# Batch 5's x turned by four transfers in place of TensorE, and twenty steps moved up in a written-out order

## The chip, the cores and the metric

One core of a Trainium2 chip runs the whole kernel. The metric is the device time of one execution in microseconds (us). Five engines work side by side, each through its own list of instructions in order: TensorE (PE, matrix products, their results go to PSUM), VectorE (DVE), ScalarE (ACT), GpSimd (POOL), and SyncE (SP), which here only issues transfers (DMA). Engines wait for each other by semaphores.

## The reference

The kernel takes q, k and v, each 8 batches x 8 heads x 576 positions x 64, and four weight matrices. First comes an attention of two parts, then a mixing network on its result:

```
q_d, k_d, v_d = means of 4 neighbouring positions          # 144 positions
out_d  = softmax(q_d k_d^T / 8) v_d, each row repeated 4 times
out_l  = softmax(q k^T / 8 where |i - j| < 4) v             # a band
x      = out_d + out_l, heads side by side                  # 8 x 576 x 512
theta  = x @ w_theta
y      = w_tok_r @ (x * cos(theta)) + w_tok_i @ (x * sin(theta))
u      = x + y
out    = u + max(u @ w_ch, 0)
```

## The kernel before

**Order.** The kernel is a list of some 1,200 short words, ORDER (lines 57 to 97). Each word is a step: two letters for its kind, then a place (a PSUM bank, a staging slot or an engine: v is DVE, a is ACT, g is POOL). Every kind runs through its batches and chunks in turn, so the n-th `mk` of the list is known to be that of batch n // 3, chunk n % 3. This text writes it as mk 6.0: batch 6, chunk 0. Instructions get a dependency on the one before them on the same engine, so the list is the order of every engine, SP's transfers included; between engines only data and buffers order the work. A step that stands earlier in the list than another, on another engine, is not held by it.

**Steps of a batch that matter here.**

| kind | line | engine | what it does |
|---|---|---|---|
| lk, lq / lv, lw | 287 / 347 | SP | load of keys, queries / of the two halves of a chunk of v into a staging slot |
| ck, cq, cv | 295, 396 | any | cast of a staging slot to bf16 |
| tp, dk | 302, 306 | PE, SP | turns k and q (dk: by transfer, batch 7 alone) |
| ev | 312, 315 | any | puts the turned k or q in place |
| kd, qd | 321 to 335 | any | means of four (two instructions on POOL) |
| ps, ex, mk, po, nm | 482, 490, 503/505, 515, 523/524 | PE, ACT, any, PE, DVE | band scores, their exponential, the band as a mask, product with v, division |
| sd, ed, nd, xn, xd, xc | 426 to 470 | PE, ACT, PE, DVE, PE, any | the same for the means |
| xt, xa | 537, 545 | PE, DVE | turns the band's result back, adds the means' result: xT, x with channels on the partitions |
| th, cs / tt, ct, zt | 556, 561/562 / 568 to 577 | PE, ACT / PE, ACT, POOL | theta, cosine and sine for four chunks of 128 positions / for the last 64 |
| xm, zz | 595, 620 | PE, DVE | turns xT to x, 128 positions at a time (four 128x128 transposes into a PSUM bank); z = x times cosine and sine |
| dx, zz | 605, 615 | SP, DVE | the same for batches 6 and 7: one DMA transpose for each of the four blocks of channels (128x512, all positions), into halves of two staging slots; zz then reads SBUF |
| dz | 581 | SP | the last 64 positions of z by DMA transpose |
| mx, ua | 636, 641 | PE, DVE | nine products over positions; u = x + y in uT, eight pieces to a batch |
| du, ut | 645, 656 | SP, any | uT turned to ur by four DMA transposes; the last 64 positions kept aside |
| ch, rl, st | 666, 674, 680 | PE, DVE, SP | u @ w_ch; max(., 0) + ur into an output buffer; its store |
| ht, rt, ss, sr | 700 to 709 | PE, DVE, SP | the same for the last 64 positions of two batches at a time, two stores |

PSUM has eight banks. A step of TensorE names one or two, and waits until their last reader is done.

**Which batches take the DMA transposes** is line 46, and the two staging slots of each are read from the list's dx words: DXS holds them, and dx i goes to the slot i // 2 names.

```
XDMA = (6, 7)
def dx(b, i, w):
    x = (DXS[b][i // 2] > DXS[b][1 - i // 2])
    dc = 2 * x + i % 2
```

**Around the change.** SP's list near the middle of the last third reads, before: du 4.0, st 2.2, st 2.3, ss 1, st 3.0, du 4.1, st 3.1, dz 5, lw 7.3, lv 7.4, du 4.2, du 4.3, lw 7.4, st 3.2, dx 6.0. SP takes them one by one: a transfer that has to wait for its data holds all behind it. rl 4.0 on DVE needs all of du 4.

Of the kernel before, what the change touches and what calls it, by code (L numbers as in the profile page):

```python
# [42 lines left out]

NSTG = 16

XDMA = (6, 7)

RPE = (0, 1, 2, 3)
ZPE = (0, 1, 2, 3)
# [23 lines left out]
rl ckg ckg cvg cvg ch3 sd67 xt45 mkg ed rl ex ts mx0 xa xt67 po45 lv5 th1 cs xa nm ua tp23 th7 up4 up1 ucv xt56 xa mkv  # L73
lv4 ch0 eva po56 po23 cvg lq2 tt4 uca th1 cs th7 nm st nm xm2 lqb rl lq1 zz lqd ct cvg xm6 lw cqg ch5 cs zz cs cqa te
up0 up1 rl sd23 ucv po67 ch4 nm rl ch0 rl ucv tp67 lv7 ed cvg pv45 vdv lk8 lk9 eva st st tp23 eva xm0 ztg lk0 lka lw
xm1 zz zz zp7 ch6 zca lvc lv3 kdg nd45 xn nd23 ckg tp01 cva xn qdg utg mx7 cka ps23 rl kdg eva ps01 ua po45 mx6 up7 ex
ex lw lw lv8 nm qdg lw cqg po45 cqg ucv lvb lv2 lw sd23 sd01 lv5 ed mx7 lw lw ua tp23 nm xd4 ed ckg ckg xca st evv
tp01 eva mx6 mkg xt45 xt23 ua ua cva cvg cvg xt01 cka ts cvg xa xa mx7 th6 xa po45 nm pv23 tt0 th1 lk4 xm4 st st mkg
th5 vdv st cs nd23 ua zz ct cqg cqg ztg tp67 th4 cs dt po01 cs cs te xn evv po23 mx5 kdg qdg xm4 xm6 mx7 nm ps01 ex nm
ps23 ua lvd ua ex ch5 ps01 ex qdg zz lw lw xm7 zz rl kdg zp6 zz mkg nd23 xn lv1 lva lv3 mx5 zca sd67 lw ps01 ex po34  # L80
mx2 ua lw ed tp01 sd67 cva nm po34 eva cvv cvg ed lw up5 uca ua mx2 cvg nm cvg lvc xd3 ua pv04 xcv lk7 lk0 mx7 lq9 lq6
lq2 lqd lq8 lqb lq5 ckg ckg vda lq7 lw xt56 mkv cqg cqg po34 lk4 xt01 xa xa ch2 st cva ts lv6 th5 up6 ckg xm0 nm th1
tp34 cs ucv cs mkg rl eva mx6 ua ua th1 xt67 lk0 lk1 cs cqa po45 mkv xa nm ht3 rt tp67 th1 eva zz xm2 lv9 xm3 xm4 lw
lve zz zz ckg dk4 kdv mx0 cqg tp67 nd23 xn cs zz ua cqa eva mx1 nd67 xn cqa sr cqa cka tt2 ct dkb up4 cva cva ua mx0
mx7 ua cvg cvv uca te po01 nm qdg kdg qdg sd56 ed po23 ua ch4 rl xd0 ch1 ztg lw nm up7 ch4 uca xca po23 dz xt67 rl evg
ckg nm st st pv15 vda mx0 ps23 xa ex rl up1 up7 evg ua ucv mx6 uca ss ps01 ex xt45 cqa utg xa ua lv1 dk4 ps23 ex mx7
up0 uca th4 lvb sd56 mkv po23 lw lw xt01 utg dt ua dk7 cvv nm th7 du ed ts evg nd56 xa nd23 tt0 xn xn ct qdg mkv mkg
evv mx1 ztg xd2 up0 ua cs ch3 rl cs te mx4 ch7 qdg ps56 rl xcv ua mx1 ex cvg po23 po45 ua uca ps67 ex ht1 nm nm st st
rt cva ss mx0 ua po67 xt45 nm ps23 st xa ex ts du kdg th1 xm0 xm7 cs th6 cs xm4 zz zz zz ch5 rl kdg mx7 ua th0 po67 nm
cs te xt45 xa sd12 ch3 xm0 ch7 ch4 xt56 st ed sd12 mkg mkg ed ts zz dz lw mx0 lv1 du du cvv lw cvg th1 cs rl uta mx3  # L90
st rl rl xa dxb ua po45 po67 pv02 nm nm ua du mx1 vda ch4 dx mkg ua po23 po01 po67 rl sr nm mx5 ua mx4 tt5 dx1 du nm
nm nd23 xn nd01 st mx6 th7 mx2 cs xn xd3 mx0 ua ua xcv ua ua xt67 utv ct dx st st xt45 xt23 xa ch1 rl th0 ch6 ch1 ch7
cs xa xa tt0 zz zz th2 th3 cs st du du ch4 rl zz zz ztg ct dz rl mx2 mx0 mx1 cs ua ua st dxe dx ht0 ua th1 cs th3 dx7
dx zz st st mx2 rl mx1 ua ua cs zz dt mx3 mx1 mx2 zz zz ztg dz mx7 ua mx3 du du du mx6 rt ua ua utg ua st rl du st mx7
mx4 ua ua ua sr mx7 mx6 mx5 ua ua ua du du ua ch7 ch6 ss ch5 rl rl ch7 ch6 ch4 ch3 du du st uta dt sta rl st rl ht7
ch2 sta rl st rl sta rl st rt ssa sr rl sta rm su k0
# [4 lines left out]
def kernel(  # L101
# [490 lines left out]
    def xm(b, c, w):  # L592
        ps = at["xm", b, c] = bank16(w)[:, 0:DM]
        for dc in range(4):
# [3 lines left out]
    DXS = {b: [int(w[2:], 36) for w in ORDER.split() if w[:2] == "dx" and w[2:]][2 * i:2 * i + 2]  # L598
           for i, b in enumerate(XDMA)}
    stg16 = stga.bitcast(BF16)  # L600
# [12 lines left out]
    def zz(b, c, w):  # L613
        if b in XDMA:
            nc.vector.tensor_tensor(out=z[b % 2][:, 2 * c:2 * c + 2, :].rearrange("p r (k e) -> p r k e", k=2),
                                    in0=dxr(b, c).unsqueeze(1).to_broadcast([P, 2, 2, 256]),
                                    in1=cs[(4 * b + c) % NCS].rearrange("p r (k e) -> p r k e", k=2), op=ALU.mult)
            return
        x = at.pop(("xm", b, c))
        nc.vector.tensor_tensor(out=z[b % 2][:, 2 * c:2 * c + 2, :],  # L620
                                in0=x.unsqueeze(1).to_broadcast([P, 2, DM]),
                                in1=cs[(4 * b + c) % NCS], op=ALU.mult)
# [185 lines left out]
```

## Time and profile before

| what | us |
|---|---|
| three timed runs: median, lowest, highest | 231.33, 229.91, 231.4 |
| profiled execution: its span, the only time given of it | 232.2 |
| TensorE busy | 217.7 |
| DVE busy | 187.7 |
| ACT busy | 156.2 |
| POOL busy | 145.0 |
| granted TensorE clock, mean of the span | 0.993 of full |

A row of the profile's timeline reads: start in us from the span's start, duration in us, engine, line of the kernel, operation, output <- inputs, sizes, how many instructions are merged in the row; and in brackets the idle time of the engine just before it and what ended that. A row of the waits reads: the engine and line that waited, who ended it, then the sum in us, how often, the longest. A row of the chain: start, duration, what. SPq is SP's queue of transfers; for a transfer the duration is that of its issue on SP, not that of the data.

### The profile page before, as it was taken

The numbers are of one execution on the slowest core, as the hardware profiler recorded it, in microseconds if no ns is written. First come the engines' busy times: TensorE is split into PE (matmuls) and PEld (weight loads), VectorE is DVE, ScalarE is ACT, GpSimd is POOL, SyncE is SP. The second block draws the span as 40 slices with busy tenths as digits, with TensorE's granted clock in tenths as the row PEclk, the third lists the DMA queues.
The fourth block names the chain that finished last, engine by engine and source line by source line (L and its number), as shares of the span: only waits on it lengthen the run. The fifth ranks groups of instructions, "written<-read, shape, count | busy, mean of one in ns | idle before, by whom it ended". The sixth has DMA issues, their size and how long they took to land.

```text
span 232.2 us, 9404 instructions
## 1 busy us (share of the span) xinstructions
PE 217.7 (94%) x3943; PEld 152.6 (66%) x3970; DVE 187.7 (81%) x367; ACT 156.2 (67%) x243; POOL 145.0 (62%) x192
## 2 busy tenths in 40 slices
PE   7997899999999999899999989989998999999992
PEld 3655678877877666776775675756655775668741
DVE  5699888999988799789968887698986978558473
ACT  4589799689988898898877978778788232430000
POOL 7689977879985999879963489598952001100000
PEclk9999799999999999999999999999999999999999
DMA  6999968997999689968999996892284358656587
GB/s 217 395 390 390 291 114 238 361 300 118 265 391 179 165 245 285 243 142 214 205 165 347 307 213 115 206 153 92 67 149 109 71 127 193 138 159 137 142 227 245
DMA packets 76795, 49.41 MB, mean 213 GB/s; under 512 B 61136, under 2 KB 61392, under 8 KB 76752
## 3 DMA queue, kind: packets, MB, share of 16 engines
q1 hardware_dynamic: 76096, 47.76, 81.9%
q10 hardware_dynamic: 656, 1.05, 1.3%
q8 instruction: 31, 0.51, 0.9%
q14 instruction: 12, 0.10, 0.1%
HBM read 33.98 MB, written 9.44 MB: 187 GB/s over the span
## 4 chain that ended last, share of the span: by engine, by line
PE 60%; DMA 10%; POOL 10%; issue 6%; ACT 5%; DVE 4%; SPq 4%; DVEq 0%; POOLq 0%; ACTq 0%
PE PS L636 21%; PE PS L666 9%; PE PS L556 8%; DMA st<-in_q_dram 6%; PE PS L302 4%; POOL two L329 3%; PE PS L515 2%; SPq L347 2%; DMA st<-in_k_dram 2%; PE PS L537 2%; DMA ur<-uT 2%; POOL q_tm L295 2%; PE PS L482 2%; PE PS L447 1%; PE PS L595 1%
## 5 line engine op out<-in xcount | busy, mean ns | idle before, releaser
L636 PE MATMUL PS<-WT,z 128*128 128x288 bf16 x576 | 78.0, 287 | 0.0
L636 PEld LDWEIGHTS <-z 128*128 128x128 bf16 x576 | 53.9, 98 | 15.9 <-issue 1.3
L641 DVE TENSOR_TENSOR uT<-PS,xT 128x288 bf16<-128x288 f32 x64 | 28.6, 452 | 12.7 <-PE PS L636 10.9
L561 ACT ACTIVATE cs<-PS,pihc 128x512 bf16<-128x512 f32 x32 | 22.0, 689 | 21.1 <-PE PS L556 13.4
L556 PE MATMUL PS<-wth,xT 128*128 128x512 bf16 x116 | 30.8, 383 | 0.7 <-issue 0.2
L666 PE MATMUL PS<-wch,uT 128*128 128x512 bf16 (+1 forms) x122 | 29.8, 373 | 0.9 <-issue 0.6
L524 DVE TENSOR_TENSOR tmp<-PS,rl 128x512 bf16<-128x512 f32 x40 | 27.7, 692 | 1.4
L545 DVE TENSOR_TENSOR xT<-PS,xdT 128x928 bf16<-128x928 f32 (+1 forms) x24 | 22.3, 952 | 3.7 <-PE PS L537 2.3
L674 DVE SCALAR_TENSOR_TENSOR osb<-PS,ur 128x512 f32<-128x512 f32 x28 | 19.1, 687 | 7.1 <-DMA ur<-uT 3.0
L490 ACT ACTIVATE pm<-PS 128x1024 bf16<-128x1024 f32 (+1 forms) x24 | 20.5, 880 | 6.2 <-PE PS L482 6.1
L577 POOL TENSOR_TENSOR zT<-xT,cst 128x512 bf16<-128x512 bf16 x7 | 9.7, 1383 | 20.6 <-ACT cst L574 20.6
L295 POOL CAST k_tm<-st 128x576 bf16<-128x576 f32 x23 | 15.1, 668 | 11.2 <-DMA st<-in_k_dram 11.1
L396 POOL CAST v_w<-st 128x512 bf16<-128x512 f32 x21 | 13.3, 651 | 10.6 <-DMA st<-in_v_dram 10.5
L770 ACT ACT_TABLE_LOAD x15 | 19.2, 1283 | 0.3
L666 PEld LDWEIGHTS <-uT 128*128 128x128 bf16 x132 | 11.9, 98 | 11.2
L562 ACT ACTIVATE cs<-PS 128x512 bf16<-128x512 f32 x32 | 19.1, 597 | 0.0
L556 PEld LDWEIGHTS <-xT 128*128 128x128 bf16 x128 | 11.7, 99 | 10.6 <-issue 0.6
L295 POOL CAST q_tm<-st 128x576 bf16<-128x576 f32 x23 | 15.4, 686 | 4.9 <-DMA st<-in_q_dram 4.7
L503 POOL TENSOR_TENSOR pm<-pm,band 128x512 bf16<-128x512 bf16 x16 | 18.3, 1164 | 0.0
L329 POOL TENSOR_TENSOR two<-qT 128x576 f32<-128x576 bf16 x14 | 16.5, 1177 | 0.7 <-ACT qT L315 0.4
L620 DVE TENSOR_TENSOR z<-PS,cs 128x1024 bf16<-128x1024 bf16 x24 | 15.8, 684 | 0.5 <-ACT cs L562 0.3
L437 ACT ACTIVATE pd<-PS 128x864 bf16<-128x864 f32 x16 | 13.8, 889 | 2.5 <-PE PS L426 2.5
(124 smaller groups left out, 422.9 us busy)
## 6 DMA issues: line engine op xcount, KB each, us to landing
st<-in_k_dram SPq DMA_DIRECT2D x32, 288.0 KB, 6.5
st<-in_q_dram SPq DMA_DIRECT2D x32, 288.0 KB, 6.3
st<-in_v_dram SPq DMA_DIRECT2D x70, 128.0 KB, 5.2
out_dram<-osb SPq DMA_DIRECT2D x26, 256.0 KB, 4.0
st<-in_v_dram SPq DMA_DIRECT2D x4, 288.0 KB, 3.5
st<-in_moe_w_tok_r_dram SPq DMA_DIRECT2D x4, 288.0 KB, 6.5
st<-in_moe_w_tok_i_dram SPq DMA_DIRECT2D x4, 288.0 KB, 7.2
st<-in_moe_w_theta_dram SPq DMA_DIRECT2D x4, 256.0 KB, 6.7
```

Source lines behind the costliest of these rows:

```text
L295: COPY[w](out=to, in_=of)
L329: nc.gpsimd.tensor_tensor(out=t, in0=src[:, :, 0:2], in1=src[:, :, 2:4], op=ALU.add)
L490: nc.scalar.activation(out=pm[(3 * b + u) % NPM][:, :, 0:n].rearrange("p e c j w -> p e (c j w)"), in_=at.pop(("ps", b, u))[:, :, 0:4 * W ...
L524: nc.vector.tensor_tensor(out=tmp[(NCH * b + c) % NTMP].rearrange("p g (j d) -> p g j d", d=D), in0=ps[:, :, :, 0:D], in1=r.unsqueeze(3).t ...
L545: nc.vector.tensor_tensor(out=xT[b % 2][:, :, lo:lo + cnt].rearrange("p e (m j) -> p e m j", j=4), in0=at.pop(("xt", b, u))[:, :, 0:cnt].r ...
L556: nc.tensor.matmul(out=ps, lhsT=xT[b % 2][:, dc, P * c:P * c + P], rhs=wth[:, dc, :], start=(dc == 0), stop=(dc == 3))
L561: nc.scalar.activation(out=t[:, 0, :], in_=ps, func=AF.Sin, bias=pihc, scale=1.0)
L562: nc.scalar.activation(out=t[:, 1, :], in_=ps, func=AF.Sin, bias=0.0, scale=1.0)
L636: nc.tensor.matmul(out=ps, lhsT=z[b % 2][:, j, P * dc:P * dc + P], rhs=WT[:, j, cols], start=(j == 0), stop=(j == 8))
L641: nc.vector.tensor_tensor(out=uT[b % 2][:, dc, cols], in0=at.pop(("mx", b, i)), in1=xT[b % 2][:, dc, cols], op=ALU.add)
L666: nc.tensor.matmul(out=ps[:, cols], lhsT=uT[b % 2][:, dc, P * c:P * c + P], rhs=wch[:, dc, cols], start=(dc == 0), stop=(dc == 3))
L770: nc.scalar.activation(out=idle, in_=pihc, func=TABLE[kind])
```

## The change

Batch 5 is added to XDMA. With that its four xm steps on TensorE (xm 5.0 to 5.3, 16 transposes) go, four dx steps (dx 5.0 to 5.3) are added on SP, into staging slots 2 and 13, and zz 5.0 to 5.3 read those slots in place of PSUM banks. dx 5.0 to 5.3 stand in one row, between st 2.3 and du 4.1.

```
-XDMA = (6, 7)
+XDMA = (5, 6, 7)
...
-evv mx1 ztg xd2 up0 ua cs ch3 rl cs te mx4 ch7 qdg ps56 rl xcv ua mx1 ex cvg po23 po45 ua uca ps67 ex ht1 nm nm st st
-rt cva ss mx0 ua po67 xt45 nm ps23 st xa ex ts du kdg th1 xm0 xm7 cs th6 cs xm4 zz zz zz ch5 rl kdg mx7 ua th0 po67 nm
-cs te xt45 xa sd12 ch3 xm0 ch7 ch4 xt56 st ed sd12 mkg mkg ed ts zz dz lw mx0 lv1 du du cvv lw cvg th1 cs rl uta mx3
...
+evv mx1 cvg ztg xd2 up0 ua cs ch3 rl cs te mx4 ch7 qdg ps56 rl xcv ua mx1 ex po23 po45 ua uca ps67 ex ht1 nm nm st st
+rt cva dx2 dx dxd dx du lw lv1 lw st st ss du mx0 ua po67 xt45 nm ps23 xa ex ts kdg th1 cs th6 cs zz zz zz ch5 rl kdg
+mx7 ua th0 po67 cvv nm cs te xt45 xa sd12 ch3 ch7 ch4 xt56 ed sd12 mkg mkg ed ts zz dz mx0 du mkg cvg th1 cs rl uta
...
```

The other lines of the list change in the same way. What they amount to, engine by engine (all else keeps its place; TensorE's list only loses xm 5):

| engine | moved |
|---|---|
| ACT | ev 5.0 (first half of k) ahead of ck 5.2 |
| POOL | mk 5.0 in place of mk 5.1, ahead of ck 6.3; cq 6.3 and qd 6.0 ahead of ck 7.1 and cv 6.3; qd 7.0 ahead of the ev of the second half of k of batch 7; cv 7.1 ahead of zt 5; mk 7.2 ahead of cv 7.4 |
| DVE | mk 5.1 in place of mk 5.0; mk 6.0 ahead of xa 5.1 and ua 4.1; cv 7.3 ahead of nm 6.4, xa 6.1 and zz 5.3; xa 6.2 ahead of rl 4.0 and rl 4.1; zz 6.2 and zz 6.3 ahead of rl 5.0 |
| SP | after st 2.3: dx 5.0 to 5.3, du 4.1, lw 7.3, lv 7.4, lw 7.4, st 3.0, st 3.1, ss 1, du 4.2, dz 5, du 4.3, st 3.2 |

More of the change, by code (lines that the diff above doesn't have):

```diff
@@ L75 @@
 up0 up1 rl sd23 ucv po67 ch4 nm rl ch0 rl ucv tp67 lv7 ed cvg pv45 vdv lk8 lk9 eva st st tp23 eva xm0 ztg lk0 lka lw
-xm1 zz zz zp7 ch6 zca lvc lv3 kdg nd45 xn nd23 ckg tp01 cva xn qdg utg mx7 cka ps23 rl kdg eva ps01 ua po45 mx6 up7 ex
+xm1 zz zz zp7 ch6 zca lvc lv3 kdg nd45 xn nd23 ckg tp01 cva xn qdg utg mx7 eva cka ps23 rl kdg ps01 ua po45 mx6 up7 ex
 ex lw lw lv8 nm qdg lw cqg po45 cqg ucv lvb lv2 lw sd23 sd01 lv5 ed mx7 lw lw ua tp23 nm xd4 ed ckg ckg xca st evv
@@ L81 @@
 mx2 ua lw ed tp01 sd67 cva nm po34 eva cvv cvg ed lw up5 uca ua mx2 cvg nm cvg lvc xd3 ua pv04 xcv lk7 lk0 mx7 lq9 lq6
[L82 to L85, printed above, removed]
@@ L86 @@
-ckg nm st st pv15 vda mx0 ps23 xa ex rl up1 up7 evg ua ucv mx6 uca ss ps01 ex xt45 cqa utg xa ua lv1 dk4 ps23 ex mx7
-up0 uca th4 lvb sd56 mkv po23 lw lw xt01 utg dt ua dk7 cvv nm th7 du ed ts evg nd56 xa nd23 tt0 xn xn ct qdg mkv mkg
-evv mx1 ztg xd2 up0 ua cs ch3 rl cs te mx4 ch7 qdg ps56 rl xcv ua mx1 ex cvg po23 po45 ua uca ps67 ex ht1 nm nm st st
-rt cva ss mx0 ua po67 xt45 nm ps23 st xa ex ts du kdg th1 xm0 xm7 cs th6 cs xm4 zz zz zz ch5 rl kdg mx7 ua th0 po67 nm
-cs te xt45 xa sd12 ch3 xm0 ch7 ch4 xt56 st ed sd12 mkg mkg ed ts zz dz lw mx0 lv1 du du cvv lw cvg th1 cs rl uta mx3
@@ L91 @@
-st rl rl xa dxb ua po45 po67 pv02 nm nm ua du mx1 vda ch4 dx mkg ua po23 po01 po67 rl sr nm mx5 ua mx4 tt5 dx1 du nm
+lq2 lqd lq8 lqb lq5 ckg mkg ckg vda lq7 lw xt56 mkv cqg cqg po34 lk4 xt01 xa xa ch2 st cva ts lv6 th5 up6 ckg xm0 nm
+th1 tp34 cs ucv cs rl eva mx6 ua ua th1 xt67 lk0 lk1 cs cqa po45 mkv xa nm ht3 rt tp67 th1 eva zz xm2 lv9 xm3 xm4 lw
+lve zz zz cqg qdg ckg dk4 kdv mx0 tp67 nd23 xn cs zz ua cqa eva mx1 nd67 xn cqa sr cqa cka tt2 ct dkb up4 cva cva ua
+mx0 mx7 ua cvg cvv uca te po01 nm kdg qdg sd56 ed po23 ua ch4 rl xd0 ch1 ztg lw nm up7 ch4 uca xca po23 dz xt67 rl evg
@@ new lines @@
+ckg nm st st pv15 vda mx0 ps23 xa ex rl up1 up7 evg ua ucv mx6 uca ss ps01 ex xt45 cqa utg mkv xa ua lv1 dk4 ps23 ex
+mx7 up0 uca th4 lvb sd56 po23 lw lw xt01 utg dt ua dk7 cvv nm th7 du ed ts qdg evg nd56 xa nd23 tt0 xn xn ct mkv mkg
+evv mx1 cvg ztg xd2 up0 ua cs ch3 rl cs te mx4 ch7 qdg ps56 rl xcv ua mx1 ex po23 po45 ua uca ps67 ex ht1 nm nm st st
+rt cva dx2 dx dxd dx du lw lv1 lw st st ss du mx0 ua po67 xt45 nm ps23 xa ex ts kdg th1 cs th6 cs zz zz zz ch5 rl kdg
+mx7 ua th0 po67 cvv nm cs te xt45 xa sd12 ch3 ch7 ch4 xt56 ed sd12 mkg mkg ed ts zz dz mx0 du mkg cvg th1 cs rl uta
@@ L92 @@
+mx3 st xa dxb rl rl ua po45 po67 pv02 nm nm ua du mx1 vda ch4 dx ua po23 po01 po67 rl sr nm mx5 ua mx4 tt5 dx1 du nm
 nm nd23 xn nd01 st mx6 th7 mx2 cs xn xd3 mx0 ua ua xcv ua ua xt67 utv ct dx st st xt45 xt23 xa ch1 rl th0 ch6 ch1 ch7
-cs xa xa tt0 zz zz th2 th3 cs st du du ch4 rl zz zz ztg ct dz rl mx2 mx0 mx1 cs ua ua st dxe dx ht0 ua th1 cs th3 dx7
+cs xa xa tt0 zz zz th2 th3 cs st du du ch4 zz zz rl ztg ct dz rl mx2 mx0 mx1 cs ua ua st dxe dx ht0 ua th1 cs th3 dx7
 dx zz st st mx2 rl mx1 ua ua cs zz dt mx3 mx1 mx2 zz zz ztg dz mx7 ua mx3 du du du mx6 rt ua ua utg ua st rl du st mx7
```

## Prediction

> **What bounds the kernel now.** I read the page first, then who waits for whom on TensorE from 108 us on (the stretch that the edits reach), then the engines in order of time around each wait found. Steps are named kind, batch, index: po 6.0 is the po step of batch 6, chunk 0. A row is matched to its step by counting the steps of that line along the order list.
>
> ```profile
> span 232.2 us, 9404 instructions
> PE 217.7 (94%) x3943; PEld 152.6 (66%) x3970; DVE 187.7 (81%) x367; ACT 156.2 (67%) x243; POOL 145.0 (62%) x192
> ```
>
> TensorE is busy for 94% of the span. So from 108 us on the time falls only where TensorE's list gets shorter or where one of its few idle pieces goes. The idle pieces, by who ended them:
>
> ```profile
> PE PS L515 <- DVE pm L505: 0.8, 1, 0.8
> PE PS L302 <- POOL q_tm L295: 0.8, 1, 0.8
> PE PS L515 <- DVE osb L674: 0.4, 1, 0.4
> PE PS L515 <- DVE xT L545: 0.3, 1, 0.3
> PE PS L426 <- POOL qd L335: 0.3, 1, 0.3
> ```
>
> These five are 2.6 us. I leave out the rest of that answer, pieces put down to issue, of which no edit is the cause. Every number below is set against the profiled 232.2 us; the median of the timed runs, 231.33 us, lies 0.9 us below it, and a gain counted in the profile is taken off that median.
>
> **The change part by part.** *tp 6.1 (the second half of q), 0.81 us, and sd 6, 0.3 us.* TensorE waits for a cast that POOL makes behind another cast, ck 7.1, for which a key load lands late.
>
> ```profile
> 121.08 4.92 SPq L287 DMA_DIRECT2D st<-in_q_dram  x8
> 121.08 4.99 DMA st<-in_q_dram
> 134.20 0.66 POOL L295 CAST k_tm<-st 128x576 bf16<-128x576 f32 x1 [3.83 <-DMA st<-in_k_dram]
> 135.53 0.68 PE L302 MATMUL PS<-ident,q_tm 128*128 128x128 bf16 x9 [0.81 <-POOL q_tm L295]
> ```
>
> POOL's 134.20 cast is ck 7.1, and cq 6.3 stands behind it. The load of cq 6.3 is the fourth of the eight issues from 121.08, so out by about 124.0 at the latest (four issues at the mean of 0.62 us end at 123.5); the first landed 4.99 us after its issue, which puts the fourth near 129, five microseconds before it is used. The new list puts cq 6.3 and qd 6.0 ahead of ck 7.1, into the 3.83 us in which POOL stands. The 0.81 us go; qd 6.1, which ended the 0.3 us wait, comes earlier too, as qd 6.0 has then been done in the idle time. mk 5.0 and mk 5.1 change engines, each into the other's kind of place: no TensorE wait of the list above is on either, so nothing.
>
> *po 6.0, 0.83 us.* It waits for mk 6.0 on DVE.
>
> ```profile
> 150.54 1.12 DVE L545 TENSOR_TENSOR xT<-PS,xdT 128x928 bf16<-128x928 f32 x1 [1.34 <-PE PS L482]
> 151.94 1.88 DVE L505 TENSOR_TENSOR pm<-pm,band 128x1024 bf16<-128x1024 bf16 x1
> 157.81 0.68 DVE L505 TENSOR_TENSOR pm<-pm,band 128x1024 bf16<-128x1024 bf16 x1
> 151.10 2.18 POOL L312 COPY kT<-st 128x1152 bf16<-128x1152 bf16 x1 [2.58 <-DMA st<-k_tm]
> 153.88 0.32 PE L515 MATMUL PS<-v_w,pm 64*64 64x65 bf16 x16 [0.83 <-DVE pm L505]
> ```
>
> The same form takes 0.68 us for mk 6.1 and 1.88 us here: it starts inside POOL's copy, which ends at 153.28, and ends 0.54 us after that. The new list has mk 6.0 ahead of xa 5.1, in DVE's idle 1.34 us, before that copy starts. The 0.83 us go. What may still hold it there is qd 7.0, moved into POOL's 2.58 us; but po 6.0 asks only at about 153, some three microseconds after mk 6.0 can start.
>
> *The sixteen transposes, 0.89 us.*
>
> ```profile
> 167.22 0.61 PE L595 MATMUL PS<-ident,xT 128*128 128x128 bf16 x8
> 167.67 1.03 PE L556 MATMUL PS<-wth,xT 128*128 128x512 bf16 x4
> 168.53 0.39 PE L595 MATMUL PS<-ident,xT 128*128 128x128 bf16 x4
> 168.75 1.03 PE L666 MATMUL PS<-wch,uT 128*128 128x512 bf16 x4
> ```
>
> From start to start eight take 0.45 us and four take 0.22 us; the last four (xm 5.3) are priced like these, 0.22: 0.89 us of a busy TensorE. The Trainium skill ("VectorE: DVE Perf Modes", The three transpose paths and Rules for kernel authors) advises against this edit: it gives 390 ns for a 128x128 on TensorE, 1309 ns on the transfer path, and says to use TensorE where PSUM will do. By that figure sixteen would free 6.2 us, an estimate that this trace's 0.22 us per four does not bear out.
>
> *The four transfers on SP's queue, and the wait behind them.* They stand behind st 2.3 and ahead of du 4.1, lw 7.3, lv 7.4, lw 7.4, st 3.0, st 3.1, ss 1, du 4.2, dz 5, du 4.3.
>
> ```profile
> 155.60 0.61 DVE L545 TENSOR_TENSOR xT<-PS,xdT 128x448 bf16<-128x448 f32 x1
> 155.66 1.98 SPq L680 DMA_DIRECT2D out_dram<-osb  x2
> 165.81 0.54 SPq L709 DMA_DIRECT2D out_dram<-osb  x1
> 167.03 1.28 SPq L645 DMA_TRANSPOSE ur<-uT  x1
> 170.85 1.34 SPq L347 DMA_DIRECT2D st<-in_v_dram  x2
> 172.24 2.62 SPq L645 DMA_TRANSPOSE ur<-uT  x2
> 173.66 4.26 DMA ur<-uT
> 178.04 1.29 DVE L674 SCALAR_TENSOR_TENSOR osb<-PS,ur 128x512 f32<-128x512 f32 x2 [2.11 <-DMA ur<-uT]
> 179.91 0.45 PE L515 MATMUL PS<-v_w,pm 64*64 64x65 bf16 x31 [0.34 <-DVE xT L545]
> 198.29 5.92 SPq L605 DMA_TRANSPOSE st<-xT  x4
> DMA to landing us min/median/max: 2.4/3.0/4.1
> ```
>
> SP stands from 157.64 to 165.81, since ss 1 waits for DVE's rt 1 and everything else for batch 4 is behind ss 1. The transfers need the whole xT of batch 5, which xa 5.2 completes at 156.21, so they fill that gap: four took 5.92 us for batch 7 (the last two rows; the landing row is line 605's own). Then, in the old clock, 157.64 + 5.92 = 163.56; du 4.1 1.28, the three v halves 3 x 0.67, st 3.0 and 3.1 1.98 as st 2.2 and 2.3 took, ss 1 0.54, du 4.2 1.31, dz 5 1.28 as du 4.1: du 4.3 is reached at 172.0. Before, it was issued at 173.66 and landed 4.26 us later. Now it lands at 176.2 even with that, 1.7 us earlier. DVE's rl 4.0 stands idle 2.11 us for it until 178.04, and that is what TensorE's po 7.0 waits on (0.4 + 0.3 us: rl 4.1, and xa 6.2 behind it). The new list also puts xa 6.2 ahead of rl 4.0. What is late next is DVE itself, which was free for rl 4.0 at 175.93 (178.04 - 2.11) and comes to it at 176.5 with xa 6.2 (0.6 us) done: both rl end 1.29 us later, at 177.8. TensorE, which asked about 0.7 us before 179.91, asks 0.89 us earlier now, at 178.3. The 0.7 us go.
>
> *ev 5.0 ahead of ck 5.2: nothing.*
>
> ```profile
> 95.61 0.46 PE L482 MATMUL PS<-qT,kT 64*64 64x64 bf16 x32 [0.60 <-ACT kT L315]
> 95.23 0.69 DVE L674 SCALAR_TENSOR_TENSOR osb<-PS,ur 128x512 f32<-128x512 f32 x1 [0.93 <-DMA out_dram<-osb]
> 96.64 0.69 DVE L524 TENSOR_TENSOR tmp<-PS,rl 128x512 bf16<-128x512 f32 x1
> 97.56 0.32 PE L515 MATMUL PS<-v_w,pm 64*64 64x65 bf16 x16
> ```
>
> The 0.60 us go there, but rl 1.2 on DVE still waits for a store until 95.23, nm 3.3 behind it still ends at 97.33, and po 3.4, which takes over its PSUM pair, can start only 0.2 us earlier. Without that cover it would be worth 0.6 us; that end goes into the range.
>
> *zz 5 from SBUF.* Its operands were PSUM and SBUF, now both are SBUF, and POOL is at work on mk 7 then.
>
> ```profile
> 166.77 4.49 POOL L503 TENSOR_TENSOR pm<-pm,band 128x512 bf16<-128x512 bf16 x4
> 169.71 0.69 DVE L620 TENSOR_TENSOR z<-PS,cs 128x1024 bf16<-128x1024 bf16 x1 [0.33 <-ACT cs L562]
> 195.60 1.28 DVE L615 TENSOR_TENSOR z<-st,cs 128x1024 bf16<-128x1024 bf16 x2
> ```
>
> From PSUM it ran undisturbed beside POOL (0.69 us); from SBUF it takes 0.64 us with POOL idle; beside POOL no row shows it. The nearest row is mk 6.0 above: such a multiply stands until POOL's instruction ends. Per zz the cost is between 0 and one POOL piece, 4.49 / 4 = 1.12 us. A gain is excluded, since undisturbed times are alike. zz 5.2 has 0.33 us of cover. I take one half piece, 0.56 us, that reaches TensorE through rl 3.2 (xt 6.1 takes its PSUM bank).
>
> Sum: 0.81 + 0.3 + 0.83 + 0.89 + 0.7 - 0.56 = 2.97 us, in the profile 232.2 - 3.0 = 229.2, in the timed median **228.3 us**. After po 7.0 the lists of TensorE, and SP's queue from du 5.0 on, are paced by TensorE's own mx steps, so what is won by then is kept.
>
> **The rivals.** *The port.* zz 5.0 and zz 5.2 each stand a full piece: 2.24 - 0.33 = 1.9 us late, and TensorE's xt 6.1 with them. The gain left is 3.5 - 1.9 = 1.6 us, 229.7 us. For it: mk 6.0's 1.88 us, and POOL goes back to back for 4.49 us. Against it: waits that were won earlier shift DVE and POOL alike, and once DVE has its turn it made mk 6.1 and the next copy in a row. The Trainium skill ("SBUF — State Buffer", Who interferes with whom) has a rule for it: a DVE instruction with two SBUF inputs and a POOL instruction that reads SBUF exclude each other for the whole of the one that is first. The row of mk 6.0 agrees.
>
> *Other waits take their place.* The first three edits win nothing lasting, for instance as batch 7's loads, set by SP, hold the casts: only 0.89 + 0.7 are left, 229.7 us. For it: POOL's 3.83 us is a load's landing, and that does not move. Against it: of the five waits only the two of batch 6 stand behind that landing, and the new list takes them out from behind it.
>
> *Slower: the queue.* If SP stood at each transfer until it has landed, four would take 4 x 4.1 = 16.4 us in place of 5.92, and du 4.3 would go 10.5 us later, at 182.5; landed 4.26 us later, 186.7, it holds rl 4.0 8.7 us longer than before, of which the 1.94 us won earlier come off: +6.8, 238.1 us. It decides from 9.6 us for the four on (du 4.3 then lands 1.94 us later than before, which is no change); with the median 3.0 each, 12.0 us, it gives +2.4, 233.7 us. Against it: batch 7's four were issued in 5.92 us, less than two landings.
>
> That the change does not do what it says is no case here: the switch drops the four xm steps from the list and turns zz's operand with them.
>
> **How the numbers follow.** About 1%, 2.3 us, is what can be told from no change: 229.0 to 233.6. The forecast, with the gain between 2.3 and 4.1 us (0.6 more from ev 5.0, none lost at the port), gets 0.60 and is faster. The port gets 0.20 and the other waits 0.14, both within 1%. The queue gets 0.06, slower by more than 1% in most of it. With a little of the rivals on the better side: faster 0.61, same 0.34, slower 0.05. The range runs from 231.33 - 4.1 = 227.2, a little under for the spread of single runs, 227.0, up to 230.9, past both rivals at 229.7 by the 1.2 us at which their worst pieces meet; 0.13 is left above and 0.06 below.
>
> **What would show it.** In the profile after: no wait of TensorE on q_tm near 134 us; mk 6.0 at 0.7 us and no wait of po 6.0; no L595 between 160 and 180 us; the four L605 before ss 1, in about 5 to 6 us; du 4.3 landing before DVE reaches rl 4.0; po 7.0 about 3 us earlier. The port would show as line 615 rows of over 1 us beside POOL's L503 and as idle time of TensorE ahead of xt 6.1 (L537). What would make me wrong: cv 7.3, now ahead of nm 6.4 on DVE, standing for its load lw 7.3; or a later stage that does not keep what po 7.0 wins.

## The result and the profile after

Six timed runs of the changed kernel have a median of 233.46 us (232.46 to 234.0), six of the kernel before, on the same chip, 229.91 us (229.21 to 231.4). The ratio is 1.0127 with a 95% interval of 1.0092 to 1.0163: the change makes the kernel slower by 1.3%, 2.1 to 3.7 us. The forecast was 228.3 us, and the range ended at 230.9. (The ratios in this text are taken over fast executions and need not be the quotients of the medians beside them.)

The page of the changed kernel, and who waits for whom on TensorE from 108 us on (engine, line, who ended the wait, then us, times, longest):

```profile
span 230.7 us, 9407 instructions
PE 218.5 (95%) x3954; PEld 151.2 (66%) x3954; DVE 187.9 (81%) x367; ACT 156.1 (68%) x243; POOL 146.2 (63%) x192
```

```profile
PE PS L515 <- DVE uT L641: 1.9, 1, 1.9
```

All five waits of before are gone. The steps behind four of them, tp 6.1, mk 6.0, po 6.0 and po 7.0, from the timeline:

```profile
134.28 0.67 PE L302 MATMUL PS<-ident,q_tm 128*128 128x128 bf16 x9
...
147.44 0.69 DVE L505 TENSOR_TENSOR pm<-pm,band 128x1024 bf16<-128x1024 bf16 x1
...
151.26 0.30 PE L515 MATMUL PS<-v_w,pm 64*64 64x65 bf16 x16
...
177.59 0.45 PE L515 MATMUL PS<-v_w,pm 64*64 64x65 bf16 x32
```

None waits, and mk 6.0 takes 0.69 us in place of 1.88. But one wait has come: a po step (line 515) stands 1.9 us for a ua step of DVE (line 641). And the profiled span is 1.5 us shorter than that of before (232.2), although the timed runs are longer. Both facts turn out to matter. The rows around the new wait, from the timeline of the changed kernel:

```profile
155.13 5.16 SPq L605 DMA_TRANSPOSE st<-xT  x4
162.53 2.00 SPq L347 DMA_DIRECT2D st<-in_v_dram  x3
163.48 5.46 POOL L503 TENSOR_TENSOR pm<-pm,band 128x512 bf16<-128x512 bf16 x4
168.90 1.60 POOL L505 TENSOR_TENSOR pm<-pm,band 128x512 bf16<-128x512 bf16 x1
165.67 3.81 DVE L615 TENSOR_TENSOR z<-st,cs 128x1024 bf16<-128x1024 bf16 x3 [0.26 <-DMA st<-in_v_dram]
169.41 0.68 DVE L674 SCALAR_TENSOR_TENSOR osb<-PS,ur 128x512 f32<-128x512 f32 x1
170.01 0.44 DVE L641 TENSOR_TENSOR uT<-PS,xT 128x288 bf16<-128x288 f32 x1
168.39 0.21 PE L515 MATMUL PS<-v_w,pm 64*64 64x65 bf16 x1
170.50 0.32 PE L515 MATMUL PS<-v_w,pm 64*64 64x65 bf16 x15 [1.90 <-DVE uT L641]
```

The four transfers are issued in 5.2 us, well ahead of need. Then zz 5.0 to 5.2 (line 615) take 3.81 us in a row, beside POOL's mk 7.0, 7.1 and 7.2 (lines 503 and 505). In the old form, from PSUM, they took 1.28 + 0.69 us with 0.33 us between them; the first two, in the trace of the kernel before:

```profile
168.10 1.28 DVE L620 TENSOR_TENSOR z<-PS,cs 128x1024 bf16<-128x1024 bf16 x2
```

Behind them on DVE stand rl 3.2 and ua 4.7, and po 6.4 on TensorE takes the PSUM bank that ua 4.7 releases. Line 615 alone, in the changed kernel:

```profile
L615 DVE TENSOR_TENSOR z<-st,cs x4: 681/1164/1647, 165.7 to 172.9; 128x1024 bf16<-128x1024 bf16 x4
```

The same instruction takes 0.68 us or 1.65 us. The two long ones, zz 5.1 and 5.2, are beside POOL and end about 0.55 us after a piece of POOL's does. zz 5.0 is beside POOL too, but it starts 0.02 us ahead of POOL's third piece and takes 0.69 us. POOL pays as well: its four pieces take 5.46 us in place of the 4.49 of before. So the two engines stand for each other in turn.

### The profile page after: what moved, and what is told of

Read it like the earlier page. It is cut to its first block, busy times and chain, and to the rows that moved or that the text cites. A ratio compares the mean times of both kernels' runs of the same rounds, so it can differ in the third digit from the quotient of the medians.

```text
span 230.7 us, 9407 instructions
## 1 busy us (share of the span) xinstructions
PE 218.5 (95%) x3954; PEld 151.2 (66%) x3954; DVE 187.9 (81%) x367; ACT 156.1 (68%) x243; POOL 146.2 (63%) x192
## 4 chain that ended last, share of the span: by engine, by line
PE 74%; DMA 6%; DVE 6%; POOL 5%; ACT 4%; issue 2%; SPq 0%; DVEq 0%; POOLq 0%; ACTq 0%
PE PS L636 27%; PE PS L556 11%; PE PS L666 9%; PE PS L302 5%; DMA st<-in_q_dram 3%; PE PS L515 2%; PE PS L537 2%; POOL two L329 2%; PE PS L447 2%; PE PS L764 2%; PE PS L482 2%; DVE z L615 2%; DMA utr<-ut 2%; PE PS L595 2%; PE PS L568 2%
## 5 line engine op out<-in xcount | busy, mean ns | idle before, releaser
L556 PE MATMUL PS<-wth,xT 128*128 128x512 bf16 x128 | 31.8, 379 | 0.0
L666 PE MATMUL PS<-wch,uT 128*128 128x512 bf16 (+1 forms) x132 | 31.2, 373 | 0.5 <-POOL wch L243 0.5
L503 POOL TENSOR_TENSOR pm<-pm,band 128x512 bf16<-128x512 bf16 x16 | 19.2, 1226 | 0.0
L329 POOL TENSOR_TENSOR two<-qT 128x576 f32<-128x576 bf16 x14 | 16.0, 1145 | 4.4 <-ACT qT L315 4.2
L329 POOL TENSOR_TENSOR two<-kT 128x580 f32<-128x580 bf16 x13 | 15.0, 1152 | 0.6 <-ACT kT L315 0.2
L315 ACT COPY kT<-PS 128x1152 bf16<-128x1152 bf16 x11 | 12.3, 1121 | 3.8 <-PE PS L302 3.3
```

What stands on the lines that cost most here:

```text
L329: nc.gpsimd.tensor_tensor(out=t, in0=src[:, :, 0:2], in1=src[:, :, 2:4], op=ALU.add)
L503: EW[w].tensor_tensor(out=t[:, x], in0=t[:, x], in1=m[:, x], op=ALU.mult)
L556: nc.tensor.matmul(out=ps, lhsT=xT[b % 2][:, dc, P * c:P * c + P], rhs=wth[:, dc, :], start=(dc == 0), stop=(dc == 3))
L666: nc.tensor.matmul(out=ps[:, cols], lhsT=uT[b % 2][:, dc, P * c:P * c + P], rhs=wch[:, dc, cols], start=(dc == 0), stop=(dc == 3))
```

## The experiments

For each kernel the table gives the time between the ends of steps on DVE, from its one trace: E is the start to ua 2.0; then the stretches ua 2.0 to ua 3.7, to rl 3.1, to ua 4.6, to ua 4.7, to nm 7.0, to ua 7.7; and the sum from ua 2.0 on. Every edit but ev 5.0's lies behind ua 2.0; E varies between 94.3 and 97.5 us among kernels that are, but for ev 5.0, the same there. So traces are compared by the sum, and times by the ratio to the kernel before.

| kernel | E | to ua 3.7 | to rl 3.1 | to ua 4.6 | to ua 4.7 | to nm 7.0 | to ua 7.7 | sum |
|---|---|---|---|---|---|---|---|---|
| before, the trace of the prediction | 96.29 | 46.55 | 19.31 | 4.17 | 5.06 | 9.84 | 39.41 | 124.34 |
| before (e0) | 96.80 | 45.10 | 18.67 | 4.17 | 5.06 | 9.81 | 39.41 | 122.23 |
| before (e11) | 95.80 | 45.11 | 17.71 | 4.17 | 5.06 | 10.00 | 39.41 | 121.47 |
| before (e12) | 97.46 | 45.09 | 17.72 | 4.17 | 5.06 | 9.79 | 39.41 | 121.25 |
| changed | 96.22 | 45.35 | 17.71 | 4.25 | 6.91 | 8.45 | 39.41 | 122.08 |
| changed (e4) | 95.17 | 45.25 | 17.71 | 4.22 | 8.10 | 8.45 | 39.40 | 123.14 |
| changed (e13) | 96.50 | 45.52 | 17.72 | 4.17 | 8.03 | 9.98 | 39.41 | 124.84 |
| changed (e14) | 95.64 | 45.19 | 17.71 | 4.17 | 8.03 | 10.02 | 39.41 | 124.53 |
| moves only (e7) | 94.33 | 45.19 | 17.72 | 4.17 | 5.18 | 8.87 | 39.41 | 120.53 |
| moves only (e1) | 95.12 | 45.19 | 17.61 | 4.17 | 5.15 | 8.78 | 39.41 | 120.31 |
| moves only (e9) | 96.28 | 45.23 | 17.61 | 4.17 | 5.17 | 8.86 | 39.40 | 120.45 |
| transfers only (e2) | 94.33 | 45.23 | 17.70 | 4.17 | 7.49 | 12.96 | 39.41 | 126.97 |
| cv 7.4 ahead of mk 7.0 (e3) | 94.72 | 45.24 | 17.61 | 4.17 | 5.61 | 8.45 | 39.40 | 120.49 |
| the same, near slots (e8) | 96.89 | 45.19 | 17.76 | 4.17 | 5.06 | 8.45 | 39.40 | 120.03 |
| changed, near slots (e10) | 96.02 | 45.19 | 17.61 | 4.17 | 6.93 | 10.07 | 39.40 | 123.37 |
| stand added (e6) | 96.84 | 45.20 | 17.69 | 4.17 | 7.26 | 8.61 | 39.41 | 122.33 |
| transfers further ahead (e5) | 94.32 | 45.20 | 17.61 | 5.82 | 6.01 | 8.45 | 39.41 | 122.50 |

The theories: that the gains of the prediction were in one execution only (against: they are real and something larger eats them); that zz 5 from SBUF is locked out by POOL; that TensorE's stand costs more than its length, through the granted clock; and that the slots which the transfers were given add a wait of their own.

### The kernel before, again

The first kernel is the one before, without any edit, timed and traced once more; the later two executions, e11 and e12, were each timed once.

> The kernel before, unchanged, for a second trace of it. Theory A (the trace the prediction was read from is a late execution, and its waits of TensorE at 134, 153 and 179 us are not those of most executions): the ratio is 1.00, the span of most runs lies 227 to 230 us, and the new trace lacks at least two of the three waits (0.81, 0.83 and 0.7 us). Theory B (the waits are always there, and the change loses more than them elsewhere): the same three waits stand in the new trace within 0.3 us each.

Ratio 1.003 (0.9987 to 1.0074), so the comparison itself is even. TensorE's waits from 108 us on in this trace, issue left out:

```profile
PE PS L515 <- DVE pm L505: 0.6, 1, 0.6
...
PE PS L515 <- DVE osb L674: 0.4, 1, 0.4
PE PS L515 <- DVE xT L545: 0.3, 1, 0.3
```

tp 6.1's 0.8 us and sd 6's 0.3 us are not there; of the three waits that the expectation names, one is gone and two stay, so neither theory's condition is met in full. This execution took 232.33 us with a span of 230.6, so the device time is the span and about 1.7 us more; the changed kernel's is the same (232.46 and 230.7). The span of 232.2 on which the prediction was built then belongs to an execution of about 233.9 us, later than every one of the three timed runs of 229.91 to 231.4.

> The kernel before, for a third trace: which waits are in its executions. Theory E (the waits at tp 6.1 and po 6.0 come and go from one execution to the next, the one at po 7.0 is in all): no wait of TensorE at tp 6.1, between 0 and 0.8 us at po 6.0, 0.7 us at po 7.0; from ua 2.0 to ua 7.7 it takes 121 to 122.3 us (124.3 and 122.2 in the two traces so far).

> As e11: a fourth trace of the kernel before. Theory E: from ua 2.0 to ua 7.7 121 to 122.3 us, the 0.7 us at po 7.0 again.

230.6 and 232.03 us. All waits of TensorE in e11 from 108 us on:

```profile
PE PS L515 <- DVE osb L674: 0.5, 1, 0.5
PE PS L515 <- DVE xT L545: 0.3, 1, 0.3
```

e12 has 0.3 and 0.3. So po 6.0's wait for mk 6.0 is 0.83, 0.6, 0 and 0 us in four executions of one kernel, and the two of tp 6.1 and sd 6 are in one of four. Only po 7.0's, 0.6 to 0.8 us, is in all. The stretch to ua 3.7 is 45.1 us in all three later traces of this kernel, against the 46.55 of the prediction's.

### The moves alone

The changed kernel with batch 5's x on TensorE, as before:

```
-XDMA = (5, 6, 7)
+XDMA = (6, 7)
...
-rt cva dx2 dx dxd dx du lw ...
+rt cva du lw ...
...
-... th1 cs th6 cs zz ...
+... th1 xm0 xm7 cs th6 cs xm4 zz ...
...
-... sd12 ch3 ch7 ...
+... sd12 ch3 xm0 ch7 ...
```

> The twenty moves without the transfers: batch 5's x stays on TensorE. Theory A (the waits that the moves take away are not there in most executions): ratio 0.995 to 1.01. Theory C (the moves do win their 1.9 us and the transfers lose more): ratio 0.985 to 0.993. Theory D (the loss comes from the moves): ratio 1.01 to 1.015, as for the whole change.

> e1 again, on the same chip as e4 to e6. All theories: ratio 0.990 to 1.000. Theory E (the moves take away waits that are only in part of the executions of the kernel before, at po 6.0, and one that is in all, at po 7.0): 0.5 to 1.5 us under the kernel before, and a narrower spread of its times.

> The moves alone (e1, e7) once more, beside e8 and e10: ratio 0.992 to 0.999. It is the measure for e8: if TensorE's shorter list is worth anything once port and slots are out of the way, e8 lies under it.

Ratios 0.9974 (0.9934 to 1.0014), 0.9948 (0.9907 to 0.9989) and 0.9943 (0.9911 to 0.9975): the moves gain 0.3 to 0.6%, 0.6 to 1.3 us (e1's interval reaches no change, those of the other two do not). TensorE has no wait left from 108 us on but pieces put down to issue. By the traces the sum is 120.31, 120.53 and 120.45 us, a mean of 120.43, against 121.36 for e11 and e12 (e0, where po 6.0 still waits 0.6 us, has 122.23). Those 0.93 us lie in the one stretch from ua 4.7 to nm 7.0, 8.8 to 8.9 us for 9.8 to 10.0: that of po 7.0.

### The transfers alone

```
-XDMA = (6, 7)
+XDMA = (5, 6, 7)
...
-rt cva ss mx0 ua po67 xt45 nm ps23 st xa ex ts du kdg th1 xm0 xm7 cs th6 cs xm4 zz zz zz ch5 rl kdg mx7 ua th0 po67 nm
-cs te xt45 xa sd12 ch3 xm0 ch7 ch4 ...
+rt cva dx2 dx dxd dx ss mx0 ua po67 xt45 nm ps23 st xa ex ts du kdg th1 cs th6 cs zz zz zz ch5 rl kdg mx7 ua th0 po67 nm
+cs te xt45 xa sd12 ch3 ch7 ch4 ...
```

> The four transfers in place of the sixteen transposes, in the old order of everything else. Theory C (the loss comes with the transfers: zz 5.1 and zz 5.2 stand for POOL's mk 7 pieces, 1.6 us each, and TensorE's po 6.4 stands 1.9 us behind them): ratio 1.005 to 1.02, and line 615 rows over 1.2 us beside POOL's L503. Theory D (loss from the moves): ratio 0.99 to 1.00.

236.15 us, ratio 1.0281 (1.0191 to 1.0371). The two long waits of TensorE and, below them, rows of its timeline:

```profile
PE PS L515 <- DVE osb L674: 2.5, 1, 2.5
PE PS L515 <- DVE uT L641: 2.5, 1, 2.5
```

```profile
163.22 4.74 DVE L615 TENSOR_TENSOR z<-st,cs 128x1024 bf16<-128x1024 bf16 x3
173.50 2.61 SPq L645 DMA_TRANSPOSE ur<-uT  x2
178.72 1.29 DVE L674 SCALAR_TENSOR_TENSOR osb<-PS,ur 128x512 f32<-128x512 f32 x2 [2.50 <-DMA ur<-uT]
```

The loss comes with the transfers, not with the moves: zz 5.0 to 5.2 take 4.74 us here, and po 6.4 stands 2.5 us for ua 4.7. The other 2.5 us stand at po 7.0, behind du 4.2 and 4.3, which SP issues from 173.50 on. Ahead of them in the old order is lw 7.3, and SP's own waits show that it stood there:

```profile
SPq L347 <- DVE z L615: 6.1, 1, 6.1
```

lw 7.3 is issued at 172.12, just after zz 5.3 ends. It writes slot 11, which lies between the two slots that zz 5.3 reads; the section on the slots below shows the same dependency the other way round. In the changed kernel lw 7.3 stands ahead of zz 5, and rl 4.0 there waits for nothing: the moves do what the prediction said on SP's queue, and transfers into these slots need them.

### The changed kernel, again

> The changed kernel, unchanged, for a second trace and beside e5 to e7 on one chip. Theory C (the port: TensorE stands 1.9 us behind zz 5.1 and zz 5.2) with theory G (such a stand makes the granted clock fall to a half for 3.4 us in part of the executions, which costs up to 1.7 us more): ratio 1.008 to 1.016, the 1.9 us wait within 0.4 us, and more executions with a mean granted clock under 0.992 than the kernel before has. If the loss were from the state of the chip in the first comparison: ratio 0.995 to 1.003.

> The changed kernel, for a third trace. Theory C: zz 5.0 to 5.2 take 3.3 us or more and TensorE stands 1.5 us or more at po 6.4. Theory G: if the granted clock falls to a half it does so within 4 us after that stand, and from ua 4.7 to nm 7.0 it then takes about 10 us in place of 8.45.

> As e13: a fourth trace of the changed kernel, with the same numbers by theories C and G.

232.93 us for e4, ratio 1.0126 (0.9977 to 1.0275), and single executions of 235.39 and 233.74 us for e13 and e14. TensorE's wait for ua 4.7 is 3.1, 3.0 and 3.0 us. The rows of line 615 in e4, e13 and then e14:

```profile
164.93 4.56 DVE L615 TENSOR_TENSOR z<-st,cs 128x1024 bf16<-128x1024 bf16 x3 [0.70 <-DMA st<-in_v_dram]
```

```profile
166.59 4.39 DVE L615 TENSOR_TENSOR z<-st,cs 128x1024 bf16<-128x1024 bf16 x3 [0.80 <-DMA st<-in_v_dram]
```

```profile
165.24 4.54 DVE L615 TENSOR_TENSOR z<-st,cs 128x1024 bf16<-128x1024 bf16 x3 [0.66 <-DMA st<-in_v_dram]
```

So the profile shown as "after" is the mildest of four. The mean of the four sums is 123.65 us. That is 2.3 over the 121.36 of e11 and e12, 2.0 over the three later traces of before and 1.3 over all four of them; the times say 2.9 (2.1 to 3.7).

In e13 and e14, and not in the other two, the stretch after the stand is longer as well, 10.0 us for 8.45. Stretches of e13: us, then busy time of each engine with its count of instructions, the granted clock, the share of the DMA and GB/s.

```profile
168.96:172.37 3.41, 0.39 (x46) 0.37 (x46) 3.41 (x6) 2.57 (x4) 2.49 (x2) 1.00 0.40 83
172.37:175.79 3.42, 3.42 (x45) 1.38 (x30) 3.26 (x6) 0.89 (x1) 0.00 (x0) 0.50 0.39 115
175.79:179.20 3.41, 3.41 (x46) 1.92 (x45) 1.82 (x4) 1.62 (x2) 0.00 (x0) 1.00 0.02 5
```

After a stretch of 3.41 us in which TensorE was busy for 0.39 us, its clock is half for just 3.41 us.

### Taking POOL away from zz 5

One word of the changed list is moved: POOL's cast cv 7.4, which waits for a load, ahead of mk 7.0 to 7.2 in place of behind them. The load holds POOL while DVE does zz 5.

```
-... sd12 mkg mkg ed ts zz dz mx0 du mkg cvg th1 ...
+... sd12 cvg mkg mkg ed ts zz dz mx0 du mkg th1 ...
```

> The changed kernel with one more move: on POOL cv 7.4, which waits for a load until about 167.3 us, stands ahead of mk 7.0 and mk 7.1, so that POOL is idle while zz 5.0 to 5.2 read SBUF. Theory C (the port): zz 5.0 to 5.2 at 0.7 us each, the 1.9 us wait of TensorE at po 6.4 under 0.5 us, and 1.5 to 2 us less than the changed kernel: ratio 1.003 to 1.007. If the port is not the cause: ratio 1.01 to 1.016, as for the changed kernel.

230.52 us (lowest 228.76, the execution that was traced), ratio 1.0003 (0.9957 to 1.0048): better than the changed kernel's 1.0127, and no better than before.

```profile
164.49 1.90 DVE L615 TENSOR_TENSOR z<-st,cs 128x1024 bf16<-128x1024 bf16 x3 [0.88 <-DMA st<-in_v_dram]
166.23 0.62 POOL L396 CAST v_w<-st 128x512 bf16<-128x512 f32 x1 [4.29 <-DMA st<-in_v_dram]
166.82 4.94 POOL L503 TENSOR_TENSOR pm<-pm,band 128x512 bf16<-128x512 bf16 x4
167.40 0.32 PE L515 MATMUL PS<-v_w,pm 64*64 64x65 bf16 x15 [0.61 <-DVE uT L641]
```

With POOL idle the three take 1.90 us in place of 3.81 to 4.56 and TensorE stands 0.6 us in place of 1.9 to 3.1. Nothing of zz 5 itself was changed, so the long rows are POOL's doing. What is left is the wait ahead of zz 5.0, 0.88 us, "for a load of v".

### The slots

zz 5.0 starts 0.29 us after lw 7.3 has landed in each trace: 165.38 and 165.67 in the changed kernel, 164.20 and 164.49 in e3, 164.64 and 164.93 in e4. lw 7.3 goes to slot 11. The transfers go to slots 2 and 13, and zz reads both as one block with a stride, over all that lies between. Here they go to slots 12 and 13, once in e3's kernel and once in the changed one:

```
-rt cva dx2 dx dxd dx du lw ...
+rt cva dxc dx dxd dx du lw ...
```

> e3 (cv 7.4 ahead of mk 7.0 on POOL) with batch 5's transfers into staging slots 12 and 13 in place of 2 and 13. In three traces zz 5.0 started 0.29 us after the landing of lw 7.3, which goes to slot 11, between the two. Theory H (zz reads the two slots as one strided block, and waits for what is written to the slots in between): zz 5.0 follows xa 6.0 with no idle time, TensorE's wait at po 6.4 falls from 0.6 us to under 0.2, and the time is 0.3 to 0.9 us under e3, 0 to 1 us under e9. If it waits for its own transfers: idle time ahead of zz 5.0 as in e3 (0.9 us), time as e3.

> The changed kernel with the transfers in slots 12 and 13 and nothing else: the port is as in the changed kernel. Theory C (the port holds the most of the loss): zz 5.0 starts up to 0.7 us earlier but zz 5.0 to 5.2 still take 3.3 us or more, TensorE's wait at po 6.4 stays over 1.3 us, ratio 1.005 to 1.015. If the slots were the cause and not the port: ratio 0.995 to 1.003.

e8: 229.29 us (lowest 227.71), ratio 0.9913 (0.9881 to 0.9945), faster than before by 0.9%. Its rows:

```profile
165.79 1.28 DVE L615 TENSOR_TENSOR z<-st,cs 128x1024 bf16<-128x1024 bf16 x2
167.40 0.69 DVE L615 TENSOR_TENSOR z<-st,cs 128x1024 bf16<-128x1024 bf16 x1 [0.33 <-ACT cs L562]
168.43 0.61 POOL L396 CAST v_w<-st 128x512 bf16<-128x512 f32 x1 [4.22 <-DMA st<-in_v_dram]
```

The wait for the load is gone: it was one that the program itself had put between a write into slot 11 and a read over it, nothing of the chip. Line 615 has three semaphore waits of DVE in the changed kernel (four steps) and two in e8. TensorE's wait for ua 4.7 is no longer listed either, and the rows of zz 5 are those of the kernel before, 1.28 and 0.69 us with 0.33 between them. That 0.33 us, for a cosine of ACT (cs 5.2), is in both.

e10: 232.45 us, ratio 1.006 (1.0023 to 1.0098). The wait for the load is gone there too, but with POOL back beside it zz 5 takes 4.18 us and TensorE stands 1.9:

```profile
164.77 4.18 DVE L615 TENSOR_TENSOR z<-st,cs 128x1024 bf16<-128x1024 bf16 x3
```

Its timed runs fall into two groups, 230.34 to 230.84 us with a mean granted clock of 0.993 to 0.999, and 232.38 to 233.7 us with 0.987 to 0.993; one more took 236.87. The profiled one (233.01 us) is of the second group; its stretches:

```profile
164.37:167.78 3.41, 3.41 (x20) 1.76 (x18) 3.41 (x4) 3.13 (x6) 3.41 (x3) 1.00 0.88 259
167.78:171.19 3.41, 1.32 (x63) 0.98 (x64) 3.38 (x7) 2.97 (x5) 2.74 (x3) 1.00 0.57 123
171.19:174.60 3.41, 3.41 (x10) 1.19 (x9) 2.45 (x4) 0.58 (x1) 0.00 (x0) 0.50 0.38 114
```

The half clock again follows a stretch of little work, and again costs 1.6 us (10.07 for 8.45). The time between the two groups, some 2 us, is about that. That the groups are the executions with and without the half clock is argued from their clocks, since only one of them was traced. The mean clock alone is weak evidence: the traced execution of e9 has 0.987 with its half clocks near 25 us and after its last matrix product, and none in between.

### A stand put in by itself

The moves alone, and on DVE ahead of ua 4.7 two reductions of 1.1 us into a tile that nobody reads: the kernel computes 2.2 us of DVE work more than the reference needs.

```
-... ch5 rl kdg
+... ch5 rl zx zx kdg
...
+        if kind == "zx":
+            nc.vector.tensor_reduce(out=scr, axis=AX.X, op=ALU.add, in_=kT[0][:, 0:2, 0:448] ...)
```

> e1 (the moves alone, x turned on TensorE) with two reductions added on VectorE ahead of ua 4.7, about 1.05 us each, whose result nobody reads: TensorE stands about 1.9 us at po 6.4, as in the changed kernel, without any transfer or port. Theory G (a stand of 1.9 us costs more than itself, by the granted clock): 2.5 to 4 us over e7, and executions with a mean granted clock under 0.994. If a stand costs itself alone: 1.7 to 2.3 us over e7, clock as in e7.

231.65 us, ratio 1.0065 (1.0025 to 1.0105), beside e7's 228.69 on the same chip: 2.96 us. Its rows (lines are one higher in this kernel):

```profile
168.59 2.20 DVE L770 TENSOR_REDUCE scr<-kT 128x224 f32<-128x896 bf16 x2
170.71 0.45 DVE L642 TENSOR_TENSOR uT<-PS,xT 128x288 bf16<-128x288 f32 x1
171.21 0.32 PE L516 MATMUL PS<-v_w,pm 64*64 64x65 bf16 x15 [1.73 <-DVE uT L642]
```

No transfers, no zz from SBUF, only DVE late at ua 4.7: TensorE stands 1.73 us at the same po 6.4, and the sum in the trace is 1.8 us longer than e7's. DVE's place there is thus on the path, and most of what it is late by comes through: 1.8 of the 2.2 us. The times show 1.2 us more than the trace. The traced execution had no half clock at that place, other executions may have had it; that is not shown, and the 1.2 us stay open.

### The transfers further ahead

e3, with the four dx steps ahead of st 2.2 and st 2.3, meant to have them out of the way of the later loads:

```
-... ht1 nm nm st st
-rt cva dx2 dx dxd dx du lw ...
+... ht1 nm nm dx2 dx dxd dx st st
+rt cva du lw ...
```

> e3 with the four transfers ahead of st 2.2 and st 2.3 on SP as well, about 2 us earlier, since zz 5.0 stood 0.9 us for them in e3. Theory C: zz 5.0 no longer stands, TensorE's wait at po 6.4 falls from 0.6 us to under 0.2, ratio 0.990 to 0.999. If TensorE's shorter list is worth its 0.89 us here: 0.7 us or more under e7, the moves alone. If VectorE and ScalarE set the pace there: within 0.4 us of e7.

231.21 us, ratio 1.0053 (1.0 to 1.0105): not the gain that was expected, by the times no better than e3 (the intervals overlap), by the trace 2.0 us longer. Two waits of TensorE in it:

```profile
PE PS L556 <- DVE osb L704: 1.2, 1, 1.2
PE PS L515 <- DVE uT L641: 1.0, 1, 1.0
```

The two stores now leave 5 us later, rt 1 on DVE (line 704) waits for them to free its output buffer, and TensorE stands 1.2 us behind it. The cast cv 7.4 came sooner as well, so that POOL was back on mk 7 during zz 5.1 and 5.2, which cost 1.0 us at po 6.4. Both are known mechanisms in new places; the edit shows that SP had no 5 us to give there.

## Why the prediction was wrong, by its own steps

**What bounds the kernel.** TensorE, and the time falls only where its list is cut or an idle piece goes: held. It lacked the other half, that the same list is lengthened by a new idle piece wherever another engine is late, and that DVE has little slack at ua 4.7 (e6: 1.8 of 2.2 us added came through). That what is won by po 7.0 is kept held too: from nm 7.0 to ua 7.7 it takes 39.4 us in every trace.

**Setting the gain against the median.** This failed. "A gain counted in the profile is taken off that median" supposes that the profiled execution has the waits of the median one. It was about 233.9 us, 2.5 us above the slowest of the three timed runs, and the sum from ua 2.0 on was 124.34 us where three later ones have 121.25 to 122.23. The page's span and the list of times stood side by side; 232.2 above all three times, with a device time that can only be longer than the span, should have said so.

**tp 6.1 and sd 6, 0.81 + 0.3 us; po 6.0, 0.83 us.** The mechanism is right: with the moves these waits are gone, tp 6.1 starts without one, mk 6.0 takes 0.69 us. But they are worth that only in an execution that has them: the first two were in one of four traces, the third in two of four. So most of these 1.9 of the 2.97 us were not there to win in a middling execution. The rival "other waits take their place" came near the amount for another reason: nothing took their place, they were mostly absent.

**po 7.0, 0.7 us.** Right: 0.93 us by e1, e7 and e9. The transfers fit SP's gap (5.16 us from 155.13 for the forecast 5.92 from 157.64), and rl 4.0 waits for nothing.

**The sixteen transposes, 0.89 us.** TensorE's list is shorter by that, but e8 against the moves alone is only 0.4 us faster in the trace (120.03 for 120.43), and by the times the two can't be told apart. DVE, held by cs 5.2 of ACT for 0.33 us, sets ua 4.7, and TensorE's time won ahead of it is partly waited away: po 6.4 takes 0.59 us in e8 and 0.32 in e9. That this is where the rest went is argued, not shown. The Trainium skill ("VectorE: DVE Perf Modes", Rules for kernel authors) advises TensorE for transposes where PSUM will do; for the change as it stands that advice came out right (with e8's slots and POOL's order it is about even), though not by the page's price of 390 ns each, and by a cost that stands elsewhere: the reader of the result.

**ev 5.0, nothing.** Nothing of it is seen: the stretch to ua 2.0 scatters over 3 us with or without it. It could not be measured here.

**zz 5 from SBUF, -0.56 us.** The term that decides. The prediction allowed 0 to 1.12 us per step and took one half piece in all, because DVE, once it has its turn, had made two instructions in a row. What the runs show is 1.64 us for each of zz 5.1 and 5.2 in the changed kernel, 0.96 us more than undisturbed, twice: 1.9 us. In e4, e13 and e14 the three take 4.4 to 4.6 us, 2.5 to 2.7 more than e3's 1.90. DVE's turn did not last here: POOL's next piece came between zz 5.0 and zz 5.1. In the rows from which the prediction took its turn POOL's instruction at 157.81 (zt 5) did stand through two of DVE's, 2.76 us for the 1.15 it takes elsewhere; why DVE kept its turn there and not here is not shown. The Trainium skill ("SBUF — State Buffer", Who interferes with whom) has the two engines exclude each other for the whole of the instruction that comes first; 1.65 us beside POOL and 0.68 us without agree with it, and a step that stands for one piece each time is what it leads to; zz 5.0, which started first, took 0.69 us, and POOL's piece beside it stood. Also the place was wrong: the prediction followed rl 3.2 to xt 6.1, the wait was at the next step of DVE, ua 4.7, to po 6.4.

**The rivals.** The port had the mechanism and, in the profiled execution, the size to a tenth (1.9 us late, and TensorE with it). The size is partly luck: that profile is the mildest of four, and the two long steps are zz 5.1 and 5.2, not zz 5.0 and 5.2. Its total, 229.7 us, failed since it set 3.5 us of gains against them, of which e8 shows 1.3. The slower rival, SP standing until each transfer lands, did not happen. No rival had the granted clock, and none took the port as a way to the slower side. Of the two signs of being wrong that the prediction named, neither came: cv 7.3 starts right behind ua 4.7, and the last stretch keeps what is won.

**The sum again,** as differences between traces, ua 2.0 on (e8 is one trace): 121.36 (e11, e12), less 0.93 for po 7.0 and 0.4 for the transposes, makes the 120.03 of e8. The changed kernel adds 2.05 us in the profile after, 3.1 in e4, and 4.8 and 4.5 in e13 and e14, of which 1.6 are half clock and 0.7 to 0.8 the slots' wait. The mean of the four is 123.65, 2.3 us over e11 and e12; the times say 2.1 to 3.7.

## What to carry to other kernels

Moving an operand from PSUM to SBUF to relieve TensorE can make its reader on VectorE stand for GpSimd, 1.64 us here for 0.68: look what GpSimd does at that moment, count one whole GpSimd instruction for every VectorE instruction, and follow the delay to the PSUM bank that is released last. Before idle pieces of a trace are counted as gains, compare the span with the timed runs, and look at a second trace: waits of a few tenths come and go between executions of one kernel. Two staging slots that are read as one block should lie side by side.

## What the runs showed of the hardware

- **A short stand can halve the clock.** In e2, e10, e13 and e14 the granted clock is 0.5 for 3.41 us after TensorE had stood 1.9 to 3.0 us, which costs 1.5 to 1.6 us more in the last three (8.45 us become 9.98 to 10.07). The Trainium skill ("TensorE: Matmul & The Clock Gate", What's actually happening) tells of a window of 3413 ns, with which the 3.41 us agree. The Trainium skill (the same page, Why this matters for your kernels) advises against idle gaps over about 3 us; the runs here do not bear that out as a limit, 1.9 us in e10 was enough. The stretch before it had 1.32 us of TensorE's work in e10 and 0.39 in e13; with 1.54 us in e6 no drop followed. But in the first trace of before a drop from 24.91 to 28.32 us followed a stretch with 2.06 us, so a limit can't be read from busy time alone. That a stand which falls across two stretches goes unpunished would explain the changed kernel's trace and e4's, which have none; the least busy of their four stretches has 1.63 us of work. It is argued, not shown.
- **The start scatters.** The same work up to ua 2.0 takes 94.3 to 97.5 us. Part of it goes with the clock: five of the seventeen traces have a half clock for 3.41 us or more between 21 and 30 us, with a start of 96.3 to 97.5 us and a mean of 96.75; the other twelve have 94.3 to 96.8, with a mean of 95.4. What sets the rest was not tried.
